# First layer as seven block products in place of eight, in chunks 1 to 8 of a pooled-attention and four-expert kernel

## The chip, the cores and the metric

The kernel runs on one core of one Trainium2 chip. The metric is device time in microseconds (us) of one execution, lower is better. Times are medians of several executions. Engines are named as in the profile: PE is TensorE (matmuls), DVE VectorE, ACT ScalarE, POOL GpSimd, SP the engine that issues many of the DMAs.

## The reference, cut to what matters

```python
# attention: q, k, v are 8 x 8 x 576 x 64; keys and values are averaged by 8, so 72 of each
k_p = k.reshape(B, H, 72, 8, D).mean(axis=3);  v_p = v.reshape(B, H, 72, 8, D).mean(axis=3)
attn_out = softmax(q @ k_p.T / sqrt(D)) @ v_p
x = attn_out.transpose(0, 2, 1, 3).reshape(4608, 512)
# four experts, p = normalized domain_probs
for e in range(4):
    h = np.maximum(x @ w1[e], 0.0)            # "first layer":  4608x512 @ 512x1024
    out += p[:, e:e+1] * (h @ w2[e])          # "second layer": 4608x1024 @ 1024x512
```

The kernel cuts the 4608 tokens into nine chunks of 512: the first 512 tokens of each of the eight batches, and a ninth chunk (chunk 8) of what remains of all batches. A pair (chunk, expert) has one first and one second layer. While the layers of chunk c run, the attention of batch c+1 is worked in between them.

## The kernel before: the parts that the change touches

The second layer is already done as 7 block products in place of 8: each operand is cut into four quarters, seven products of sums of quarters are made, and the results are added with the right signs. The sums of quarters of H (the hidden layer) are made on DVE. The first layer is plain: 32 matmuls of 128x512.

```python
    def up(c, e, fcs, at=slice(0, NT)):                    # first layer, 4 matmuls for each fc
        ...
        for fc in fcs:
            h_ps = psum_h.tile([P, NT], F32, name="h_ps")
            out_ps = h_ps[:, 0:at.stop - at.start]
            for kc in range(KC):
                nc.tensor.matmul(out_ps, lhsT=w1_bf[:, e, kc, fc*P:(fc+1)*P], rhs=xT[:, kc, at], ...)
            nc.scalar.activation(out=H_sb[:, fc, at], in_=out_ps, func=ACT.Relu)

    def down(c, e, step):                                  # second layer, one of 7 products
        a11, a12, a21, a22 = quarters(c, e)
        ...
            lambda: (0, False, a11, w[:, LO, 0:HD], 0, 0, True),
            lambda: (1, False, a12, w[:, HI, 0:HD], 0, 0, False),
            lambda: (0, True, state["S2"], t[:, 1], 0, 1, True),     # the third needs a sum of H
            ...
        # 8 matmuls of 128x256, then add(): acc = p_e * PSUM + acc on DVE (ACT for e == 0)

    def turn(b, r):                                        # x of a batch, transposed by a DMA
        ...
        if b:
            nc.sync.dma_start_transpose(out=dst, in_=x_tok)
            return
        ...                                                # batch 0 alone: transposed on PE

    def next_loads(b):                                     # loads of the next batch
        ...
        turned = state[("kpT", b)][0:1, 0, 0:1] if b >= BUSY else state[("xT", b)][0:1, 0, NT - 1:NT]
        nc.gpsimd.tensor_copy(out=gate[0:1, 0:1], in_=turned)   # holds the queue until x is turned
        load_q(b + 1); load_k(b + 1); load_v(b + 1); load_q_rem(b + 1)
```

The one-element copy called `gate` matters later: it makes the GpSimd queue, which issues the loads, wait until the last transposed x of batch 1 has landed before it loads batch 2. (In the kernel before, POOL waited 35.71 us for `xT<-x_tok`, ran the copy at 75.24 and issued the first of these loads at 75.75.)

The softmax here doesn't subtract the row's maximum and nothing guards it: scores larger than these inputs give would overflow.

## Time and profile before

| | before |
|---|---|
| time, median of 3 runs | 531.21 us (530.46 to 531.53) |
| PE busy | 510.8 us of a span of 528.7 (97%) |
| DVE / ACT / POOL busy | 66% / 46% / 8% |
| DVE in a 55-us window in the middle | 39 us |
| one first layer (32 matmuls 128x512) | 32 x 0.2165 = 6.93 us |

The page of the kernel before gives the busy time of each engine and the shares of the chain of waits that ended last, by engine and by line. L450 is the first layer, L524 the second.

```profile
span 528.7 us, 9160 instructions
PE 510.8 (97%) x3735; PEld 332.7 (63%) x3802; DVE 348.8 (66%) x715; ACT 240.8 (46%) x413; POOL 40.0 (8%) x57
...
PE 87%; DVE 9%; DMA 1%; issue 1%; ACT 1%; DVEq 0%; POOL 0%; POOLq 0%
```

PE is the limit. The next lines, from the PE timeline of the kernel before (start, duration, engine, line, operation, operands, how many), show what a narrow matmul costs.

```profile
216.43 1.04 PE L450 MATMUL h_ps<-xT,w_bf 128*128 128x512 bf16 x4
217.30 1.04 PE L524 MATMUL o_ps<-w_bf,H_sb 128*128 128x256 bf16 x8
218.18 0.81 PE L450 MATMUL h_ps<-xT,w_bf 128*128 128x512 bf16 x3
```

From start to start, four matmuls of 512 columns take 0.87 us (216.43 to 217.30) and eight of 256 columns 0.88 us (217.30 to 218.18). A matmul with half the columns takes half the time, about 0.109 us.

The windows of the kernel before give busy time in stretches of the run (columns: busy us of PE, weight loads, DVE, ACT, POOL with instruction counts, then the granted TensorE clock, the DMA share and GB/s). The first is the start of chunk 1, the second the steady state.

```profile
75.00:101.00 26.00, 25.04 (x169) 16.64 (x171) 22.15 (x42) 11.31 (x21) 4.10 (x7) 1.00 0.81 141
...
211.00:266.00 55.00, 54.36 (x400) 36.12 (x406) 39.03 (x80) 25.99 (x45) 4.46 (x5) 1.00 0.55 87
```

PE has about half a microsecond to spare in 55.

To compare stretches of the two runs I use a marker: the start of the third product of a second layer, which is the same in both kernels and recurs once in each layer. These lines of the PE timeline of the kernel before are the first matmul of chunk 1, then the marker beside the first layer of chunk 1, expert 0 (I call this step 0), beside that of expert 1 (step 1), and in the very last second layer (step 32).

```profile
75.32 1.02 PE L450 MATMUL h_ps<-xT,w_bf 128*128 128x512 bf16 x4
...
80.40 1.03 PE L524 MATMUL o_ps<-wt_bf,S_943 128*128 128x256 bf16 x8 [0.79 <-DVE acc L556]
...
93.41 1.04 PE L524 MATMUL o_ps<-wt_bf,S_1081 128*128 128x256 bf16 x8
...
517.10 1.03 PE L524 MATMUL o_ps<-wt_bf,S_5909 128*128 128x256 bf16 x8 [0.91 <-DVE acc L556]
```

### The profile page before, as it was taken

The numbers are of one execution on the slowest core, as the hardware profiler recorded it, in microseconds if no ns is written. First come the engines' busy times: TensorE is split into PE (matmuls) and PEld (weight loads), VectorE is DVE, ScalarE is ACT, GpSimd is POOL, SyncE is SP. The second block draws the span as 40 slices with busy tenths as digits, with TensorE's granted clock in tenths as the row PEclk, the third lists the DMA queues.
The fourth block names the chain that finished last, engine by engine and source line by source line (L and its number), as shares of the span: only waits on it lengthen the run. The fifth ranks groups of instructions, "written<-read, shape, count | busy, mean of one in ns | idle before, by whom it ended". The sixth has DMA issues, their size and how long they took to land.

```text
span 528.7 us, 9160 instructions
## 1 busy us (share of the span) xinstructions
PE 510.8 (97%) x3735; PEld 332.7 (63%) x3802; DVE 348.8 (66%) x715; ACT 240.8 (46%) x413; POOL 40.0 (8%) x57
## 2 busy tenths in 40 slices
PE   8999999999999999999999999999999999999994
PEld 4656456666666666666666666666666666666663
DVE  4432687977866767677857784778477636664665
ACT  2665413653365335633563347334733363336330
POOL 6420020200030002000300002000000000000000
PEclk9999999999999999999999999999999999999999
DMA  9999939673192125912671329232010110010002
GB/s 188 210 210 204 141 59 204 92 109 61 31 194 33 31 51 125 115 30 51 137 92 30 61 93 123 44 60 86 9 21 20 50 41 12 0 47 36 1 0 79
DMA packets 73417, 42.02 MB, mean 79 GB/s; under 512 B 44688, under 2 KB 67216, under 8 KB 73376
## 3 DMA queue, kind: packets, MB, share of 16 engines
q0 software_dynamic: 30976, 22.11, 29.2%
q1 hardware_dynamic: 42080, 18.82, 14.8%
q8 instruction: 29, 0.48, 0.4%
q10 hardware_dynamic: 320, 0.52, 0.3%
q14 instruction: 12, 0.10, 0.1%
HBM read 45.16 MB, written 9.44 MB: 103 GB/s over the span
## 4 chain that ended last, share of the span: by engine, by line
PE 87%; DVE 9%; DMA 1%; issue 1%; ACT 1%; DVEq 0%; POOL 0%; POOLq 0%
PE h_ps L450 42%; PE o_ps L524 37%; DVE acc L556 3%; PE o_ps L541 2%; PE sc_ps L262 2%; PE c_ps L290 1%; DMA kraw<-in_k_dram 1%; DVE kraw L174 1%; PE s_ps L205 1%; DVE kraw L176 1%; DVE wt_bf L469 1%; PE w_ps L221 1%; DVE x_tok L279 1%; DVE kp_100 L184 0%; ACT expT L265 0%
## 5 line engine op out<-in xcount | busy, mean ns | idle before, releaser
L454 ACT ACTIVATE H_sb<-h_ps 128x512 bf16<-128x512 f32 (+1 forms) x296 | 173.2, 585 | 242.3 <-PE h_ps L450 226.6
L556 DVE SCALAR_TENSOR_TENSOR acc<-o_ps,p_all,acc 128x256 f32<-128x256 f32 (+1 forms) x412 | 181.8, 483 | 125.9 <-PE o_ps L524 96.1
L450 PE MATMUL h_ps<-xT,w_bf 128*128 128x512 bf16 (+1 forms) x998 | 253.2, 372 | 3.2 <-ACT xT L308 0.4
L450 PEld LDWEIGHTS <-w_bf 128*128 128x128 bf16 x1184 | 112.0, 98 | 85.0 <-issue 5.3
L524 PEld LDWEIGHTS <-H_sb 128*128 128x128 bf16 x816 | 79.8, 98 | 33.3 <-issue 3.4
L524 PE MATMUL o_ps<-w_bf,H_sb 128*128 128x256 bf16 x544 | 70.3, 273 | 1.4 <-DVE acc L556 1.2
L554 ACT ACTIVATE acc<-o_ps,p_all 128x256 f32<-128x256 f32 x72 | 30.7, 470 | 12.4 <-PE o_ps L524 7.2
L524 PE MATMUL o_ps<-wt_bf,H_sb 128*128 128x256 bf16 x272 | 35.2, 272 | 0.6 <-DVE acc L556 0.3
L265 ACT ACTIVATE expT<-sc_ps 72x1024 bf16<-72x1024 f32 x32 | 31.0, 1015 | 6.6 <-PE sc_ps L262 6.6
L450 PE MATMUL h_ps<-x_rem,w_bf 128*128 128x512 bf16 x121 | 31.7, 379 | 0.3
L279 DVE TENSOR_TENSOR x_tok<-c_ps,inv 128x512 bf16<-128x512 f32 x36 | 24.9, 691 | 1.2
L541 PE MATMUL o_ps<-w_bf,H_sb 128*128 128x512 bf16 x63 | 14.7, 379 | 0.1
L290 PEld LDWEIGHTS <-expT 72*128 72x128 bf16 x256 | 12.1, 98 | 1.7 <-DVE x_tok L279 0.2
L221 PE MATMUL w_ps<-zeros 128*128 128x512 bf16 x41 | 11.7, 425 | 1.2 <-DVE zeros L574 1.2
L541 PEld LDWEIGHTS <-H_sb 128*128 128x128 bf16 x64 | 6.1, 98 | 7.1
L278 DVE RECIPROCAL inv<-c_ps 128x8 f32<-128x8 f32 x36 | 7.1, 198 | 5.2 <-PE c_ps L343 2.9
L427 POOL COPY gate<-kpT_101 1x1 bf16<-1x1 bf16 x2 | 1.5, 736 | 96.9 <-DMA kpT_101<-kp_99 55.3
L174 DVE TENSOR_TENSOR kraw<-kraw 72x2048 bf16<-72x2048 bf16 x7 | 8.5, 1210 | 0.0
L174 DVE TENSOR_TENSOR vraw<-vraw 72x2048 bf16<-72x2048 bf16 x7 | 8.5, 1210 | 0.0
L89 POOL DMA_DIRECT2D kraw<-in_k_dram x9 | 7.6, 841 | 5.1 <-PE h_ps L450 4.7
L221 PEld LDWEIGHTS <-zeros 128*128 128x128 bf16 x42 | 4.1, 108 | 5.7 <-issue 2.3
L89 POOL DMA_DIRECT2D vraw<-in_v_dram x9 | 7.1, 795 | 0.7 <-DVE vp_106 L226 0.7
(489 smaller groups left out, 467.8 us busy)
## 6 DMA issues: line engine op xcount, KB each, us to landing
out_dram<-acc SPq DMA_DIRECT2D x32, 256.0 KB, 2.7
w_bf<-in_moe_w_dram POOLq DMA_DIRECT2D x7, 1024.0 KB, 22.5
kraw<-in_k_dram POOLq DMA_DIRECT2D x7, 576.0 KB, 12.3
vraw<-in_v_dram POOLq DMA_DIRECT2D x7, 576.0 KB, 14.2
q_sb<-in_q_dram POOLq DMA_DIRECT2D x7, 512.0 KB, 7.0
acc<-in_q_dram SPq DMA_DIRECT2D x2, 512.0 KB, 4.3
w_bf<-in_moe_w_dram POOLq DMA_DIRECT2D x2, 512.0 KB, 12.0
kraw<-in_k_dram POOLq DMA_DIRECT2D x2, 288.0 KB, 7.4
```

Of the source, the lines that this page charges most:

```text
L89: nc.gpsimd.dma_start(out=raw[:, hs], in_=src[b, hs].rearrange("h (j r) d -> j h r d", r=POOL))
L174: nc.vector.tensor_add(out=raw[:, hs, 0:4, :], in0=raw[:, hs, 0:4, :], in1=raw[:, hs, 4:8, :])
L221: nc.tensor.matmul(w_ps[:], lhsT=zeros[:, 0:P], rhs=zeros[:])
L265: nc.scalar.activation(out=expT[:, 2 * pair:2 * pair + 2].rearrange("j h a b t -> j b (h a) t"), in_=sc_ps[0:SP].rearrange("j b h (a t) -> ...
L279: nc.vector.tensor_tensor(out=x_tok[:], in0=c[:, :, :, 0:D], in1=inv[:].unsqueeze(3).to_broadcast([P, 2, NPAIR, D]), op=ALU.mult,)
L290: nc.tensor.matmul(c_ps[:, h // NPAIR, at:at + D + 1], lhsT=expT[:, h, r // 2, r % 2, :], rhs=vp[:, h, :],)
L450: nc.tensor.matmul(out_ps, lhsT=w1_bf[:, e, kc, fc * P:(fc + 1) * P], rhs=xT[:, kc, at], start=(kc == 0), stop=(kc == KC - 1),)
L454: nc.scalar.activation(out=H_sb[:, fc, at], in_=out_ps, func=ACT.Relu)
L524: nc.tensor.matmul(o_ps, lhsT=lhs[:, i, j * P:(j + 1) * P], rhs=rhs[:, i, :], start=(not grows and i == 0 and j == 0), stop=(i == HF - 1), ...
L541: nc.tensor.matmul(o_ps[:], lhsT=H_sb[:, fc, r * P:(r + 1) * P], rhs=w2_bf[:, e, fc, :], start=(fc == 0), stop=(fc == FCH - 1),)
L554: nc.scalar.activation(out=dst, in_=o_ps, func=ACT.Copy, scale=prob)
L556: nc.vector.scalar_tensor_tensor(out=dst, in0=o_ps, scalar=prob, in1=dst, op0=ALU.mult, op1=ALU.add,)
```

## The change

The intent is to save PE time: the first layer too becomes 7 products of blocks, 56 matmuls of 128x256 in place of 32 of 128x512, for the 32 pairs of chunks 1 to 8. The price is sums of blocks: four sums of x for each chunk, sixteen sums of w1 once, and relu of a sum of two products, which is made in one custom VectorE operation, relu(PSUM + SBUF), after ACT has copied the first product out of PSUM. To make room on DVE, two of the seven products of a second layer (steps 1 and 4) are accumulated by ACT and POOL, and the folding of k and v, from batch 2 on, is left to loads in four parts that add up in memory. H lives in two buffers by quarters, the buffers of x by tokens go from 4 to 3, and the `gate` is gone. The core of the diff:

```diff
+    def relu_sum(dst, ps, part):
+        nc.vector._custom_dve(TENSOR_ADD_SAT, out=dst, in0=ps, in1=part, s0=LARGEST, s1=0.0)
+
+    def up_product(c, e, unit, step):          # two units of two PSUM banks each
+        a11, a12, s3, a22 = weight_parts(e)
+        b11, t3, b21, b22 = x_parts(c)
+        s, t = wu_bf[:, e], state[("xs", c)]
+        bank, grows, lhs, rhs = [
+            (0, False, a11, b11),
+            (1, False, a12, b21),
+            (0, True, s[:, 1], t[:, 1]),       # the third needs a sum of x and a sum of w1
+            ...
+        ][step]
+        # 4 matmuls of 128x256
+        if step == 0 or step == 3:
+            nc.scalar.copy(out=part[:, 0], in_=ps)
+        elif step == 2:
+            nc.scalar.copy(out=part[:, 1], in_=ps)
+        elif step == 1:
+            relu_sum(quarter(0, 0), ps, part[:, 0])
+        ...
     def down(...):
+        if step in pooled and e > 0:
+            for j in range(BLOCKS):
+                nc.scalar.activation(out=addend[:, j], in_=ps[:, j], func=ACT.Copy, scale=prob)
+            nc.gpsimd.tensor_add(out=dst, in0=dst, in1=addend[:])
+    def load_part(b, part):
+        ...
+            if part:
+                nc.gpsimd.dma_start(out=raw[:], in_=rows, accum_op=ALU.add)
...
-        x_tok = npool.tile([P, 2, NPAIR, D], BF16, name="x_tok", bufs=4)
+        x_tok = npool.tile([P, 2, NPAIR, D], BF16, name="x_tok", bufs=3)
...
-        nc.gpsimd.tensor_copy(out=gate[0:1, 0:1], in_=turned)
...
+        sums = {(0, 2): lambda: first_weight_sums(0), (0, 7): lambda: weight_sums(0),
+                (1, 6): lambda: first_weight_sums(1), (2, 6): lambda: first_weight_sums(2),
+                (3, 5): lambda: first_weight_sums(3), (3, 7): lambda: weight_sums(3)}
...
+            if s == 2:
+                load_part(2, 1)
+            if s == 3:
+                load_q(2)
+                load_part(2, 2)
...
+        x_sums(1)
+        load_part(2, 3)
+        sums = {(0, 6): lambda: weight_sums(1), (1, 6): lambda: weight_sums(2)}
+        POOLED = (1, 4)
+        for g in range(7 * (N + 1) + 1):       # slots: 2 first-layer products, 1 second-layer product
+            t, i = divmod(g, 7)
+            if t < N:
+                up_product(*order[t], 0, i)
+            t2, i2 = divmod(g - 1, 7)
+            if 0 <= t2 < N:
+                up_product(*order[t2], 1, i2)
+            if g >= 1 and t2 <= N:
+                down(*below_of[t2], i2, t2 % 2, POOLED)
+            ...                                # hidden sums at i = 0, 1, 2; attention by slot
```

## The prediction

> **What bounds it now.** TensorE. The page gives PE 510.8 us busy of 528.7 (97%) at full granted clock; the chain of waits puts 87% of the span on PE lines, 42% on the first layer's matmuls and 37% on the second's. From the first matmul of chunk 1 (75.3 us) to the last first-layer matmul of chunk 8 (514.3) the timeline shows 54.9 us per chunk, and 55-us windows show 53.9 to 54.6 us of PE busy. DVE has 38 to 42 us in such a window, ACT 26, POOL at most 7.5.
>
> **Removed.** In the timeline four 128x512 matmuls take 0.866 us and eight 128x256 ones 0.870 us, so a 256-column product runs at 0.109 us: narrower matmuls cost nothing extra here (weight loads of 98 ns stay hidden, barely). A first layer falls from 32 x 0.2165 = 6.93 us to 56 x 0.1088 = 6.09 us, 0.84 us for each of 32 layers: about 27 us, all on the critical path. PE alone would give 504 us.
>
> **Added and moved, per chunk.** DVE gains six PSUM+SBUF relu sums for each layer. It is a custom operation with no duration in this trace; I take that of the 128x512 multiply-add out of PSUM, 748 ns, less the 0.09 us overlap seen between neighbours: 0.66 us. [...] My sum for three layers: 6 x 0.66 + 4 bf16 sums x 0.65 + 10 accumulations x 0.39 = 10.5 us; the first layer has 6 accumulations, 8.9 us; attention 6.5 us with sums of x, less the folding that accumulating DMAs take over. Total about 47 us of the expected 53: DVE goes from some 72% to about 90%. ACT goes to about 30 us (copies at 0.5 us), not a limit. POOL gets six 128x512 additions. [...]
>
> **Where it is given back.** A slot is 1.74 us of PE (two first-layer products and one second-layer product). At each turn of layer DVE has, in order: last relu, two accumulations, two hidden sums, a relu, two accumulations, then the S2 sum that the third second-layer product needs. Counted from durations above, S2 is ready about 6.2 us after the turn and PE asks at 6.1. So small stalls, about 0.2 us, and 0.7 to 1 us more in the turn where a context division (0.9 us) comes before S2, or where x sums meet a GpSimd addition. I put 1 to 2 us per chunk back (8 to 16 us), and 3 to 5 us once for weight sums of the first layer (16 x 0.69 us on DVE, partly in the overlapped prologue), the start of chunk 1 and the tail. Chunks 53 us, total 516 us (-2.9%).
>
> **Range.** 505 to 527 us, 8 in 10. Faster by over 2%: 0.72; within 2%: 0.26; slower: 0.02.
>
> **What would show it.** Right: chunk period 52 to 54 us; first-layer matmuls 256 wide at 0.109 us; PE busy near 480 us; DVE over 80%; new PE waits mostly on DVE (S2, relu sums), at the third second-layer product. Relu sum 0.7 to 0.8 us.
>
> **What would make it wrong.** A custom operation that costs over 0.9 us pushes DVE past PE (each 0.1 us is 4.8 us of DVE per chunk): then about 530 us. GpSimd additions that lock DVE out for over 1 us each. Accumulating DMAs landing late, so that POOL and with it the addend buffer and ACT wait. On the other side, if slack absorbs the turn stalls, 506 us.

The sum stays at 504 us of PE, 8 to 16 us given back in the chunks and 3 to 5 us once, for a stated total of 516 us (at their middles the terms add to 520, as said at the end). What the text says of x sums that meet an addition and a DVE that is locked out was the author's estimate; the kernel after shows one such sum at 1.49 us, against a mean of 417 ns in d1, which has no POOL additions.

## The result, and the profile after

The changed kernel took 533.39 us (median of 4 runs, 532.70 to 534.13); the kernel before, in the same rounds, 530.84 us (529.89 to 531.53). The ratio is 1.0047 with a 95% interval of 1.003 to 1.0064: within 2%, and if anything slower. A ratio here is always the mean time of one kernel's fast runs over that of the other's of the same rounds, so it is not quite the ratio of the medians. The predicted 516 us and its range of 505 to 527 missed.

The page of the kernel after, the lines that answer to those of before:

```profile
span 530.9 us, 11431 instructions
PE 499.8 (94%) x4562; PEld 407.0 (77%) x4570; DVE 435.4 (82%) x830; ACT 274.1 (52%) x513; POOL 156.2 (29%) x137
...
PE 71%; DVE 12%; DMA 11%; ACT 2%; issue 2%; SPq 0%; DVEq 0%; ACTq 0%
```

PE is busy for less time, as intended, but its share of the chain has fallen from 87% to 71%, and DMA has 11% of the chain where it had 1%. The same two windows of the kernel after:

```profile
75.00:101.00 26.00, 19.25 (x164) 14.48 (x162) 21.27 (x39) 7.86 (x14) 8.59 (x8) 0.87 0.90 91
...
211.00:266.00 55.00, 53.12 (x517) 45.45 (x517) 49.34 (x94) 29.84 (x56) 20.44 (x17) 1.00 0.68 79
```

In the steady window PE now lacks 1.9 us of 55 (before 0.6), and DVE has gone from 39 to 49 us. In the start window PE lacks 6.75 us of 26, and the granted clock was 0.87.

What PE waited for, in the kernel after (total us, times, longest):

```profile
PE o_ps L566 <- DVE S L187: 9.1, 12, 1.7
PE unit L500 <- DMA xT<-x_tok: 4.8, 1, 4.8
PE unit L500 <- DVE xs L187: 1.9, 1, 1.9
PE unit L500 <- ACT partial L514: 1.8, 2, 1.3
...
```

How long the four transposing DMAs of batch 1's x took from issue to landing, from the view of the tile `xT` (60 to 95 us), first in the kernel before, then in the kernel after:

```profile
DMA to landing us min/median/max: 2.5/2.5/2.5
...
DMA to landing us min/median/max: 3.7/8.8/9.0
```

L566 is the second layer, and its wait for `S` is at the marker, the third product. L500 is the new first layer. The PE timeline of the kernel after, at the start of chunk 1 and at the markers of steps 0, 1 and 32:

```profile
81.33 2.72 PE L500 MATMUL unit<-xT,w_bf 128*128 128x256 bf16 x12 [4.81 <-DMA xT<-x_tok]
...
87.05 0.61 PE L500 MATMUL unit<-xs,wu_bf 128*128 128x256 bf16 x4 [1.94 <-DVE xs L187]
...
91.34 1.04 PE L566 MATMUL o_ps<-wt_bf,S 128*128 128x256 bf16 x8
...
106.44 1.05 PE L566 MATMUL o_ps<-wt_bf,S 128*128 128x256 bf16 x8 [0.78 <-DVE S L187]
...
517.47 1.63 PE L566 MATMUL o_ps<-wt_bf,S 128*128 128x256 bf16 x8 [1.68 <-DVE S L187]
```

Now the run can be cut into three parts by the markers:

| part | before | after | difference |
|---|---|---|---|
| start: to the marker of step 1 | 93.41 | 106.44 | +13.0 |
| steady: step 1 to step 32, 31 layers | 423.69 | 411.03 | -12.7 |
| tail: step 32 to the end of the span | 11.6 | 13.4 | +1.8 |
| span of the profiled run | 528.7 | 530.9 | +2.2 |

(The tail is the span less the marker: 528.7 - 517.10 and 530.9 - 517.47. The three differences add to +2.1; the rest is rounding. The start holds one new first layer too, so its +13.0 is already net of 0.84 us.) So the layers did become faster, by about half of the 26 us that 31 layers of 0.84 us should give, and the start and the tail gave that back. The tail's 1.8 us seem to belong to this execution: behind the wait of 1.68 us the granted clock was 0.56 (517.47 to 520 us) and eight matmuls took 1.63 us, while the runs a1 to a3 and b1 to b3 below have the same wait of 1.68 us at this marker and then 1.05 us; in a1, for example, the tail is 11.7 us.

The relu sum, the one cost that had to be guessed, is in the groups of the kernel after (busy us, mean ns, idle before), by form, with four groups that will matter:

```profile
L481 DVE CUSTOM_DVE_ANT_0 H<-unit,partial 128x512 bf16<-128x512 f32 x192 | 130.7, 683 | 25.5 <-PE unit L500 12.6 <-ACT acc L601 11.8 <-ACT H L520 0.2
L187 DVE TENSOR_TENSOR S<-H 128x1024 bf16<-128x1024 bf16 x68 | 46.4, 682 | 0.3
L187 DVE TENSOR_TENSOR H<-H,S 128x1024 bf16<-128x1024 bf16 x34 | 32.3, 951 | 0.5 <-DVE S L187 0.5
...
L221 DVE TENSOR_TENSOR kp<-kraw 72x512 bf16<-72x512 bf16 x12 | 8.8, 772 | 0.0
```

It costs 683 ns, as hoped: less than the 748 ns of the 128x512 multiply-add out of PSUM in the kernel before, from which it had been estimated.

Two operations of the same shape, `S<-H` and `H<-H,S`, take 682 and 951 ns. Some DVE sums took longer beside a POOL addition. The DVE and POOL timeline of the kernel after, at one turn from a chunk to the next, shows such meetings:

```profile
249.23 1.54 POOL L577 TENSOR_TENSOR acc<-acc,addend 128x512 f32<-128x512 f32 x1 [4.36 <-DVE xs L187]
...
249.56 1.49 DVE L187 TENSOR_TENSOR xT<-xT 128x512 bf16<-128x512 bf16 x1
...
255.99 0.87 DVE L603 SCALAR_TENSOR_TENSOR acc<-o_ps,p_all,acc 128x256 f32<-128x256 f32 x2
256.77 0.68 DVE L187 TENSOR_TENSOR S<-H 128x1024 bf16<-128x1024 bf16 x1
257.03 1.56 POOL L577 TENSOR_TENSOR acc<-acc,addend 128x512 f32<-128x512 f32 x1 [6.26 <-DVE acc L603]
257.37 1.83 DVE L221 TENSOR_TENSOR kp<-kraw 72x512 bf16<-72x512 bf16 x2
...
257.51 1.05 PE L566 MATMUL o_ps<-wt_bf,S 128*128 128x256 bf16 x8 [0.95 <-DVE S L187]
```

The sum `xT<-xT` took 1.49 us beside a POOL addition, and the pair `kp` 1.83 us. In d1 below, which has no POOL additions, the means are 417 ns for `xT<-xT`, 415 for one `kp` and 678 for `H<-H,S`. Some texts call this lengthening exclusion; what is shown is the longer time, not how it comes about. DVE works almost without a gap from 249.2 to 257.5; the sum S arrives 0.95 us after PE wanted it. Two things are ahead of it that may not need to be: about 1.1 us that `xT<-xT` took beyond its mean in d1, and accumulations of the second layer.

### The profile page after: what moved, and what is told of

It reads as the page before. It is cut to its first block, busy times and chain, and to the rows that moved or that the text cites. A ratio compares the mean times of both kernels' runs of the same rounds, so it can differ in the third digit from the quotient of the medians.

```text
span 530.9 us, 11431 instructions
## 1 busy us (share of the span) xinstructions
PE 499.8 (94%) x4562; PEld 407.0 (77%) x4570; DVE 435.4 (82%) x830; ACT 274.1 (52%) x513; POOL 156.2 (29%) x137
## 4 chain that ended last, share of the span: by engine, by line
PE 71%; DVE 12%; DMA 11%; ACT 2%; issue 2%; SPq 0%; DVEq 0%; ACTq 0%
PE o_ps L566 30%; PE unit L500 28%; DMA xT<-x_tok 6%; DMA out_dram<-acc 5%; PE unit L448 5%; DVE acc L603 4%; DVE H L481 2%; PE unit L256 2%; DVE S L187 2%; PE o_ps L590 1%; PE att L300 1%; DVE xs L187 1%; PE att L326 1%; DVE wt_bf L187 1%; ACT expT L304 1%
## 5 line engine op out<-in xcount | busy, mean ns | idle before, releaser
L481 DVE CUSTOM_DVE_ANT_0 H<-unit,partial 128x512 bf16<-128x512 f32 x192 | 130.7, 683 | 25.5 <-PE unit L500 12.6
L577 POOL TENSOR_TENSOR acc<-acc,addend 128x512 f32<-128x512 f32 x50 | 69.4, 1387 | 278.2 <-ACT addend L575 197.8
L566 PEld LDWEIGHTS <-H 128*128 128x128 bf16 x1360 | 134.0, 99 | 18.5 <-issue 0.9
L512 ACT COPY partial<-unit 128x512 f32<-128x512 f32 x128 | 74.9, 585 | 112.2 <-PE unit L500 86.4
L500 PEld LDWEIGHTS <-w_bf 128*128 128x128 bf16 x1024 | 98.8, 98 | 23.4 <-issue 6.0
L566 PE MATMUL o_ps<-w_bf,H 128*128 128x256 bf16 x816 | 106.8, 274 | 0.3 <-DVE acc L603 0.3
L500 PE MATMUL unit<-xT,w_bf 128*128 128x256 bf16 x672 | 98.1, 276 | 7.4 <-DMA xT<-x_tok 4.8
L500 PEld LDWEIGHTS <-wu_bf 128*128 128x128 bf16 x768 | 73.0, 98 | 13.1 <-issue 2.5
L500 PE MATMUL unit<-xs,wu_bf 128*128 128x256 bf16 x512 | 77.1, 273 | 1.9 <-DVE xs L187 1.9
L566 PE MATMUL o_ps<-wt_bf,H 128*128 128x256 bf16 x544 | 71.4, 275 | 0.1
L566 PEld LDWEIGHTS <-S 128*128 128x128 bf16 x544 | 52.1, 99 | 20.7 <-DVE S L187 13.9
L514 ACT COPY partial<-unit 128x512 f32<-128x512 f32 x64 | 38.0, 594 | 21.3 <-PE unit L500 21.2
L566 PE MATMUL o_ps<-wt_bf,S 128*128 128x256 bf16 x272 | 36.0, 276 | 9.1 <-DVE S L187 9.1
L500 PE MATMUL unit<-xs,w_bf 128*128 128x256 bf16 x256 | 38.5, 273 | 0.0
L566 PE MATMUL o_ps<-w_bf,S 128*128 128x256 bf16 x272 | 35.5, 274 | 0.1
L500 PE MATMUL unit<-xT,wu_bf 128*128 128x256 bf16 x224 | 33.7, 273 | 0.0
```

The source lines that it names most:

```text
L481: nc.vector._custom_dve(TENSOR_ADD_SAT, out=dst, in0=ps, in1=part, s0=LARGEST, s1=0.0)
L500: nc.tensor.matmul(ps[:, n * HN:(n + 1) * HN], lhsT=lhs[:, kc, f:f + P], rhs=rhs[:, kc, :], start=(not grows and n == 0 and kc == 0), stop ...
L512: nc.scalar.copy(out=part[:, 0], in_=ps)
L514: nc.scalar.copy(out=part[:, 1], in_=ps)
L566: nc.tensor.matmul(ps[:, j], lhsT=lhs[:, i, j * P:(j + 1) * P], rhs=rhs[:, i, :], start=(not grows and i == 0 and j == 0), stop=(i == HF - 1),
L577: nc.gpsimd.tensor_add(out=dst, in0=dst, in1=addend[:])
```

## The experiments

The questions: (1) what makes the start late: the fewer buffers of x by tokens, the accumulating loads, loads in flight at all, or DVE's backlog of weight sums? (2) what eats half of the steady gain: S late on DVE because POOL additions lengthen DVE's sums and because of the order of work, or the stores? My theory for the start was that the transposing DMAs of x land late because loads of batch 2 are in flight, the rival that a smaller buffer count or DVE is to blame. In the list, each experiment changes the kernel after. The kernel before took 530.9 to 531.5 us (medians) in the rounds of the experiments.

### a1: four buffers of x by tokens

```diff
-        x_tok = npool.tile([P, 2, NPAIR, D], BF16, name="x_tok", bufs=3)
+        x_tok = npool.tile([P, 2, NPAIR, D], BF16, name="x_tok", bufs=4)
```

> The changed kernel with 4 x_tok buffers instead of 3 (before had 4). At the start of chunk 1 the fourth x_tok waited 5.2 us for the transposing DMA of the first one, and PE was idle 4.8 us. Buffer theory: the missing buffer is the cause, so the 5.2 us wait and most of the 4.8 us of PE idle vanish, -4 to -5 us (about 529). Rival, slow landing theory: the transposes land late (8.8 us against 2.5 before) because accumulating loads of batch 2 are in flight; then the fourth transpose starts earlier but also lands late, and the time falls by 0 to 2 us.

Measured: 531.95 us (529.20 to 533.06), ratio to before 1.0016 (0.9978 to 1.0054). The PE timeline of this run shows the start no earlier:

```profile
82.11 2.72 PE L500 MATMUL unit<-xT,w_bf 128*128 128x256 bf16 x12 [5.62 <-DMA xT<-x_tok]
```

DVE's wait for a buffer of x by tokens (5.2 us in the kernel after) is gone, and in its place DVE waits 5.2 us in all for the transposed x itself, ahead of the sums of x. The buffer wait was only a symptom of the late landing, and the buffer theory falls.

### a2: x of batch 1 transposed on PE

```diff
-        if b:
+        if b > 1:
             nc.sync.dma_start_transpose(out=dst, in_=x_tok)
             return
-        xt_ps = spare_bank()...
+        xt_ps = one_bank(b)...
```

> The x of batch 1 is transposed on PE through PSUM instead of by DMA, so that no transfer stands between attention and chunk 1. Slow landing theory: the 4.8 us of PE idle vanish, the first first-layer product starts near 77 instead of 81.3 us, minus 1.6 us of PE for 16 transposes; next it waits for the sums of x behind weight sums on DVE, so -3 to -6 us. Rival (DVE backlog alone sets the start): the third product still starts near 87 us and the time stays within 1 us.

Measured: 536.19 us (535.49 to 539.20), ratio 1.0112 (1.0082 to 1.0142): slower, a miss. The DMA wait was gone, but the four transposes now stood among PE's matmuls and each waited for its x on DVE (1.03 to 1.25 us each); the third product started at 92.44, after 3.57 us of waiting for the sums of x. DVE itself was behind. So taking the DMA away does not repair the start alone, and since it put new waits on PE, this run is no clean test of the landing.

### a3: stores by quarters

In the kernel after, a row of the output is stored after steps 5 and 6, when all of it is done, and the next chunk's first write to `acc` waits for that. Here each half is stored as soon as it is final.

```diff
-        if e == E - 1 and step in (5, 6):
-                store(c, row * BLOCKS + j)
+        if e == E - 1 and step in (1, 4, 5, 6):
+                store(c, row * BLOCKS + j, cols)
```

> Results are stored by column halves as soon as each is final, so the store that ACT's first write of the next chunk waits for (4.3 us in six waits in the trace, 1.6 us longest) is issued four steps earlier. Theory: ACT's wait for the store delays the copies of partial sums and so PE (1.3 us idle in chunk 4, 0.5 us in chunk 1); expected: these waits vanish, -2 to -5 us. Rival (the waits are hidden by other waits of the same turn of layer): no change[...].

Measured: 531.78 us (531.37 to 535.19), ratio 1.0032 (1.0 to 1.0064). The waits of ACT for the stores fell from 4.3 to 1.9 us, while PE's waits for S grew. Its median is 1.6 us below that of the kernel after, in other rounds. The stores are a small part of it.

### a4: POOL takes steps 4 and 6 in place of 1 and 4

```diff
-        POOLED = (1, 4)
+        POOLED = (4, 6)
```

> GpSimd takes the accumulations of steps 4 and 6 instead of 1 and 4: DVE has two accumulations fewer before the S2 sum at each turn of layer and two more after it. Order-of-DVE theory: the PE waits for S (9.1 us named, each some 0.16 us longer than named) shrink below 3 us, -4 to -8 us. Rival (exclusion between GpSimd additions and DVE sums is what makes DVE late): the additions of step 6 now fall onto the S sums themselves, waits for S stay or grow, time the same or up.

Measured: 526.15 us (525.52 to 527.94), ratio 0.9917 (0.9897 to 0.9937), with the same number of POOL additions. The window and two groups of this run:

```profile
156.00:211.00 55.00, 55.00 (x541) 47.74 (x540) 48.62 (x97) 33.03 (x61) 21.52 (x18) 1.00 0.65 77
```

```profile
L187 DVE TENSOR_TENSOR H<-H,S 128x1024 bf16<-128x1024 bf16 x34 | 23.1, 678 | 0.0
...
L221 DVE TENSOR_TENSOR kp<-kraw 72x512 bf16<-72x512 bf16 x12 | 4.5, 415 | 0.0
```

PE is busy in the whole window, and the slow forms are back at 678 ns (from 951) and 415 ns (from 772). This one line does two things: the POOL additions now lengthen DVE's sums by 5.8 us in place of 16.8 (worked out under d1), and the two accumulations of step 6 leave DVE just before the sum S is due. The runs don't separate the shares of the two.

### d1: no POOL accumulation at all

```diff
-        POOLED = (1, 4)
+        POOLED = ()
```

> The changed kernel without GpSimd additions: DVE does all accumulations (1.6 us more for each of three layers, 4.7 us per chunk, some 56 us of DVE per chunk: more than PE needs), and no DVE sum is held by GpSimd. If the exclusion costs more than the additions save, the time falls below 531; if DVE load and order decide, it rises to 540 to 555 us, with PE waits on DVE in every layer.

Measured: 562.06 us (557.20 to 565.07), ratio 1.0544 (1.0477 to 1.061). With no additions on POOL, `H<-H,S` took 678 ns, `xT<-xT` 417, `kp<-kraw` 415 and `xs<-xT,xs` 421, while the relu sum (681, in the kernel after 683) and the 128x256 accumulations (474, there 475), which read one operand from PSUM, stayed as they were. This gives what the POOL additions cost DVE in the kernel after: 34 x (951-678) + 12 x (772-415) + 7 x (724-417) + 14 x (497-421) ns = 16.8 us of DVE over the run, from the means of the two runs. In the same way a4 has 5.8 us. But without POOL's help DVE is overloaded: accumulations are late, so stores are late, so the next chunk waits at its first write. The ACT and the PE timeline of this run at a turn of chunk:

```profile
229.47 0.47 ACT L601 ACTIVATE acc<-o_ps,p_all 128x256 f32<-128x256 f32 x1 [4.46 <-DMA out_dram<-acc]
...
231.51 0.80 PE L500 MATMUL unit<-xT,w_bf 128*128 128x256 bf16 x4 [4.50 <-ACT partial L514]
```

So POOL's additions are worth having; where they fall decides what they cost.

### b1: only the first quarter of batch 2's k and v is loaded (wrong result)

```diff
-            if s == 2:
-                load_part(2, 1)
-                load_part(2, 2)
-        load_part(2, 3)
```

> Wrong result on purpose: of batch 2, only the first quarter of k and v is loaded; the three accumulating pairs of loads that were in flight at the start of chunk 1 are left out (batches 3 to 7 as in the changed kernel). Slow landing theory: the transposing DMAs of x land in about 2.5 us as before instead of 8.8, PE idles under 1 us instead of 4.8 and chunk 1 starts near 77; then the sums of x wait for the weight sums on DVE (ready near 83 instead of 87.6), -4 to -6 us in all. Rival (DVE backlog alone): start of the third product stays near 87, under -1 us.

Measured: 532.92 us (531.01 to 535.05), ratio 1.004 (1.0002 to 1.0078). The first line below is from the view of the tile of transposed x (stretch of batch 1), the others from the PE timeline of this run:

```profile
DMA to landing us min/median/max: 2.4/2.5/2.7
```

```profile
82.82 1.04 PE L500 MATMUL unit<-xs,wu_bf 128*128 128x256 bf16 x4 [3.58 <-DVE xs L187]
...
160.32 0.91 PE L500 MATMUL unit<-xT,w_bf 128*128 128x256 bf16 x4 [2.19 <-ACT partial L514]
...
161.88 1.91 PE L566 MATMUL o_ps<-wt_bf,S 128*128 128x256 bf16 x8
```

The landing is 2.5 us as in the kernel before (2.5), against a median of 8.8 in the kernel after, and PE no longer waits for a DMA. So the loads in flight do cause the late landing. (In d1 and e2 the profile puts the first product's wait of 5.67 and 3.46 us down to DVE, to a different operation in each that ended just then; the transposes landed late there too, with medians of 9.8 and 7.6 us.) The third product moved from 87.05 to 82.82, and the rest of the start is DVE's: 3.58 us of waiting for the sums of x. The total did not fall, against the expected 4 to 6 us. In the profiled execution, one of two near 535 us (the other two took 531.4 and 531.0), stores at two turns of chunk were late (7.0 us of store waits on ACT against 4.3) and cost two PE waits of about 2.2 us, with a granted clock of 0.83 from 155 to 165 us, around the first, behind which eight matmuls took 1.91 us in place of 1.04. Why the stores fell worse here was not looked into further.

### b2: b1 with the weight sums spread over later layers (wrong result)

```diff
-                (3, 5): lambda: first_weight_sums(3), (3, 7): lambda: weight_sums(3)}
+                (3, 7): lambda: weight_sums(3)}
-        sums = {(0, 6): lambda: weight_sums(1), (1, 6): lambda: weight_sums(2)}
+        sums = {(0, 3): lambda: weight_sums(1), (1, 3): lambda: weight_sums(2),
+                (2, 3): lambda: first_weight_sums(3)}
```

> As the run without the three pairs of loads (wrong result on purpose), and the weight sums of the first layer of expert 3 and two of the second layer move from the turns of layer to the fourth slot of the layers, where DVE has room. If both the late landing and the DVE backlog hold the start: a further -2 to -4 us against that run, sums of x ready near 80 us, and the S waits of chunk 1 (0.8 us each) shrink. If the landing alone holds it: within 1 us of that run.

Measured: 529.43 us (528.82 to 530.67), ratio 0.9981 (0.9961 to 1.0001). The third product began at 81.08, 1.7 us earlier than in b1. The sums of w1 of the last expert, queued on DVE ahead of the sums of x, are the second part of the late start.

### b3: parts loaded without accumulation (wrong result)

```diff
-                nc.gpsimd.dma_start(out=raw[:], in_=rows, accum_op=ALU.add)
+                nc.gpsimd.dma_start(out=raw[:], in_=rows)
```

> Wrong result on purpose: all partial loads write instead of accumulate; same bytes, same number of loads and waits. If accumulation itself makes the loads slow (7.1 to 7.8 us each in the median), they land sooner, transposes too, and the time falls 3 to 6 us; if it is the bytes and packets in flight (twice as many packets as before), the landing times and the time stay within 1 us.

Measured: 531.14 us (530.13 to 531.61), ratio 1.0003 (0.9985 to 1.002). PE started chunk 1 at 81.03 after 5.05 us of waiting for the DMA, much as in the kernel after (81.33 after 4.81), and the transposes landed in 8.2 us in the median (8.8 there). So it is not the adding that delays the transposes, it is the loads' being in flight, which the `gate` used to prevent. The parts themselves landed sooner without adding (those of k in 5.5 us against 7.1).

### c1: a4, a3 and the spread weight sums together

> Correct result. GpSimd takes steps 4 and 6, stores by column halves, weight sums moved to the fourth slot. The first alone gave 526.2 us. If the store wait and the weight sums each hold PE where the S sum no longer does: -4 to -8 us more, 518 to 522 us. Rival (they are hidden behind the start): within 1.5 us of 526.

Measured: 525.77 us (525.17 to 526.68), ratio 0.9906 (0.9888 to 0.9924): hardly better than a4 alone. Four weight sums in one block hold DVE up for 2.7 us, and the relu sums behind them made PE wait 1.75 and 1.40 us in the first layers of chunk 1. In the profiled runs c1 reached the marker of step 1 at 104.45, against 107.67 in a4, but its steady part was 1.1 us and its tail 1.4 us longer; the blocks are one cause of that, the rest was not traced.

### e2: a4 and a3

> Correct result. Steps 4 and 6 on GpSimd plus stores by halves; weight sums and buffers as in the changed kernel. a4_pool46 alone gave 526.15 us and still had PE waits of 0.6 and 0.2 us on ACT's copies. If the store wait still costs PE there: 523.5 to 525.5 us. If it is hidden once DVE is early: 525.5 to 526.7 us.

Measured: 525.66 us (525.16 to 527.82), ratio 0.9886 (0.9867 to 0.9904), the same as a4 within the spread. Once DVE is early, the store wait is hidden and a3 is worth nothing.

### c2 and c3: weight sums one at a time, with and without the gate

Both have a4 (with the last second layer left at steps 1 and 4), a3, a1, and the weight sums one to a slot. c2 also puts the gate back before the last two parts of batch 2, and moves batch 2's attention later to match.

```diff
-                (3, 5): lambda: first_weight_sums(3), (3, 7): lambda: weight_sums(3)}
+                (3, 7): lambda: weight_sums(3)}
...
-        sums = {(0, 6): lambda: weight_sums(1), (1, 6): lambda: weight_sums(2)}
+        sums = {}
+        for p in range(4):
+            sums[(0, 3 + p)] = lambda p=p: weight_sums(1, (p,))
+            sums[(1, 3 + p)] = lambda p=p: weight_sums(2, (p,))
+            sums[(2, 3 + p)] = lambda p=p: first_weight_sums(3, (p,))
-                down(*below_of[t2], i2, t2 % 2, POOLED)
+                down(*below_of[t2], i2, t2 % 2, POOLED if t2 < N else (1, 4))
```

```diff
 # c2 alone
         x_sums(1)
+        nc.gpsimd.tensor_copy(out=gate[0:1, 0:1], in_=state[("xT", 1)][0:1, 0, NT - 1:NT])
+        load_part(2, 2)
         load_part(2, 3)
```

> Correct result. GpSimd takes steps 4 and 6 (1 and 4 in the last layer), stores by halves, 4 x_tok buffers, weight sums one at a time in slots 3 to 6 of the first three layers, and the last two quarters of batch 2 are held back by a tiny copy that reads x of batch 1 (the gate of the kernel before), with attention of batch 2 later in chunk 1. If late landing and DVE backlog set the start and chunk 1: chunk 1 starts near 77 us, third product near 80, and chunk 1 takes 53 to 55 us instead of 59; 512 to 517 us. Rival (what is left is DVE work that has to be done somewhere in chunk 1): 520 or more.

> As the gated version without the gate and without the later attention. The landing theory expects chunk 1 to start near 81 to 82 us, 4 to 5 us later than gated, and the sum 517 to 521 us. If the gate does not matter: within 1 us of the gated one.

Measured: c2 520.67 us (520.48 to 520.98), ratio 0.9796 (0.9775 to 0.9818); c3 520.75 us (520.40 to 522.66), ratio 0.9804 (0.9777 to 0.9832). The gate does what it should for the start: in c2 PE began chunk 1 at 78.32 after waiting only 1.24 us, against 81.68 after 4.61 us in c3 (the transposes landed in 4.9 us in the median, against 8.7), and the marker of step 1 came at 98.93 against 103.64. But with the loads held back, batch 2's attention came late: from the marker of step 1 to that of step 5, chunk 1 took 59.59 us in c2 and 55.60 in c3. The gate moved the loss. In c3, the sum S of step 3 was late, and the PE timeline shows what followed:

```profile
133.11 1.86 PE L566 MATMUL o_ps<-wt_bf,S 128*128 128x256 bf16 x8 [2.06 <-DVE S L187]
```

These eight matmuls took 1.86 us in place of 1.04; the granted clock of the window from 101 to 156 us was 0.97, and 1.00 in the later windows up to 486 us. The length of the wait alone does not decide this: after 2.05 us in e1 eight such matmuls took 1.05 us, and after 1.68 us at the last marker 1.63 in the kernel after but 1.05 in a1.

### c4: c3 with the weight sums one layer earlier

```diff
-                (3, 7): lambda: weight_sums(3)}
+                (3, 7): lambda: (weight_sums(3), weight_sums(1))}
-            sums[(0, 3 + p)] = lambda p=p: weight_sums(1, (p,))
-            sums[(1, 3 + p)] = lambda p=p: weight_sums(2, (p,))
-            sums[(2, 3 + p)] = lambda p=p: first_weight_sums(3, (p,))
+            sums[(0, 3 + p)] = lambda p=p: weight_sums(2, (p,))
+            sums[(1, 3 + p)] = lambda p=p: first_weight_sums(3, (p,))
```

> Correct result. As c3_all_ungated (520.8 us), but the second layer's weight sums of expert 1 run in the 3.5 us that DVE idles before chunk 1, and the other two blocks one layer earlier, so none is left in the third layer. If DVE work limits chunk 1: the 2.1 us wait for S at the last layer of chunk 1 and the lower clock after it vanish, -2 to -4 us, 517 to 519 us. Rival (something else holds chunk 1): within 1 us of 520.8.

Measured: 517.09 us (516.23 to 518.10), ratio 0.9731 (0.9708 to 0.9753), a correct result and the fastest correct version, faster than both kernels. The PE waits, a window and two markers of this run:

```profile
PE unit L500 <- DMA xT<-x_tok: 6.0, 1, 6.0
PE o_ps L566 <- DVE S L187: 2.4, 2, 1.4
```

```profile
211.00:266.00 55.00, 55.00 (x529) 47.61 (x527) 46.91 (x93) 33.17 (x63) 21.03 (x17) 1.00 0.78 85
```

```profile
104.97 1.05 PE L566 MATMUL o_ps<-wt_bf,S 128*128 128x256 bf16 x8 [1.07 <-DVE S L187]
...
502.62 1.05 PE L566 MATMUL o_ps<-wt_bf,S 128*128 128x256 bf16 x8 [1.36 <-DVE S L187]
```

From step 1 to step 32 the 31 layers take 397.65 us, 26.0 less than before, as much as the products should give. That this agrees to the tenth is luck: in the same stretch the waits that the profile names for PE are 3.6 us in the kernel before and 1.4 in c4, so some 2 us of the 26.0 are waits. The start is still 11.6 us later than before, and the tail is 13.7 us (span 516.3).

### e1: c3 without batch 2's later parts (wrong result)

> Wrong result on purpose: c3_all_ungated with the three accumulating pairs of batch 2 left out, as in b1_no_parts2. If late landing costs the start 4 to 5 us and no later wait gives it back here: 516 to 517 us. If an earlier start is always given back in chunk 1: 519.5 to 521 us.

Measured: 516.07 us (515.56 to 516.52), ratio 0.971 (0.9694 to 0.9727), 4.7 us below c3, which differs only in those loads (it ran in other rounds; the ratios differ by 0.9%). Two lines of its PE timeline:

```profile
76.28 1.47 PE L500 MATMUL unit<-xT,w_bf 128*128 128x256 bf16 x12
...
99.41 1.05 PE L566 MATMUL o_ps<-wt_bf,S 128*128 128x256 bf16 x8 [1.07 <-DVE S L187]
```

The marker of step 1 came 4.2 us earlier than in c3 (103.64). So with DVE out of the way, the late landing costs the start between 4 and 5 us by itself. It is not the whole start: 99.41 is 7.0 us before the kernel after, and still 6.0 us behind the kernel before. In this stretch PE's named waits are all on DVE: 2.11 us for the sums of x, 1.19 and 1.07 us for S. A correct version that has both (no late landing and no late attention of batch 2) was not found in these runs.

### Chunk times of the main runs

The times of the other runs stand in their sections. The chunk times below are from the marker of step 1 to that of step 5, 5 to 9 and so on to 29, so they hold chunks 1 to 7; chunk 7 has little attention beside it.

| | us | ratio to before | chunk times by the markers |
|---|---|---|---|
| before | 530.84 | | 56.95 55.61 55.14 55.61 55.13 54.42 53.01 |
| after | 533.39 | 1.0047 | 54.43 54.87 55.77 54.82 52.60 53.36 49.30 |
| a4 | 526.15 | 0.9917 | 55.99 52.61 52.41 52.99 51.68 52.61 49.23 |
| c2 | 520.67 | 0.9796 | 59.59 52.69 51.68 52.62 53.44 52.61 49.16 |
| c3 | 520.75 | 0.9804 | 55.60 53.27 51.68 52.62 51.68 52.61 49.17 |
| c4 | 517.09 | 0.9731 | 51.69 52.79 51.68 52.62 51.68 52.61 49.16 |

## Why the prediction was wrong, point by point

- **What bounds the kernel: right.** PE, as the page and the windows say.
- **What the products save: right.** A matmul of 256 columns stayed at 0.109 us. The prediction said 0.84 us for each layer, 26.0 us for 31 of them, all on the critical path; c4 shows a steady part 26.0 us shorter (423.69 - 397.65), of which some 2 us are waits, as said there.
- **The cost on each engine: right.** The relu sum took 683 ns (the prediction reckoned with 0.66 us beside its neighbours and expected to see 0.7 to 0.8). DVE came to 49.34 us of a 55-us window, 90%, and 82% of the span; ACT to 30 us in that window.
- **Back-payment in the steady part: right in kind, in sum within its range, wrong in how it is spread.** The prediction had S late on DVE, by 0.2 us as a rule and by 0.7 to 1 us where sums of x meet a POOL addition, 8 to 16 us in all. After against c4, the steady part lost 13.4 us (411.03 - 397.65). In the middle chunks the S waits are 0.95 us at the turn of chunk and 0.49 in another layer. By the chunk table the loss is 2.7, 2.1, 4.1 and 2.2 us in chunks 1 to 4, under 1 us in the later ones. Between 107 and 502 us the PE waits that the profile names add to 9.5 us (S 6.6, partial 1.3, expT 1.0, H 0.6). The windows of the two steady parts split the 13.4: PE lacks 11.75 us in the kernel after and 1.67 in c4, which makes 10.1 of it; for the other 3.3 us PE is busy longer (399.28 against 395.98 us) with the same matmuls. Each wait also ends the overlap of about 0.17 us that neighbouring groups show (1.04 us long, 0.87 apart); for the 16 more waits that is about 2.7 us, an estimate. Because c4 changes a4, a3, a1 and the weight sums at once, it shows the size of the loss, and a4 shows that most of it beyond chunk 1 is the place of the POOL additions.
- **"3 to 5 us once for weight sums of the first layer (...), the start of chunk 1 and the tail": this is the step that failed.** It measured 14.8 us: 13.0 at the start and 1.8 in the tail, and the latter seems to be the lowered clock of this one execution, as said with the table. What the prediction had wrong is the overlap: it expected new PE waits mostly on DVE and the weight sums partly hidden in the prologue, and had no wait for a transposing DMA. The start divides so: the first matmul of chunk 1 came at 81.33 in place of 75.32 (6.0 us later, of which 4.81 are the wait for the DMA), the next part to the marker of step 0 took 10.0 us in place of 5.1 (a lowered clock, 0.50 from 81.3 to 84.1: 12 matmuls show 2.72 us where b1's same group shows 1.47; and 1.94 us for the sums of x), and the step from there to the marker of step 1 took 15.1 in place of 13.0. The prediction saw the weight sums, and did not see that the `gate`, which the change removed, had kept the transposes of x clear of other loads (landing 2.5 us before, 8.8 after). b1 shows that the loads delay the landing, b3 that the adding is not the reason, a1 that the buffers are not, e1 that it is worth between 4 and 5 us; b2 shows that the queue of weight sums is the next part (1.7 us at the third product). With both changed, and a4, a3 and a1 besides, e1 wins back 7.0 of the 13.0 us. Of the other 6.0, 4.4 us are named waits for DVE (the kernel before has 0.8 there); the rest is not split, and no run removes it.
- **The arithmetic of the prediction.** Its own terms, at their middles, add to 504 + 12 + 4 = 520 us, not 516. With the measured terms in their place, the profiled span comes out: 528.7 - 26.0 + 13.4 + 13.0 + 1.8 = 530.9; this must come out, since the terms are differences of the same markers, and is no further proof. A slip besides, which did not matter at 683 ns: with six relu sums for each layer a chunk has 24, so 0.1 us more for each would be 2.4 us of DVE per chunk and not 4.8.
- **"PE busy near 480 us" was no good test.** It measured 499.8, but even c4, with the whole steady gain, has 494.6. A matmul at a lowered clock counts as busy for longer (12 took 2.72 us at a granted clock of 0.50, against 1.47 in b1, as above); how much of the difference that is was not measured. And the busy time of the kernel before reads low: its page has 1184 weight loads of L450 but only 1119 matmuls, so some matmul records are missing.
- **The danger that was named, additions on POOL that hold DVE up: half right.** They cost 16.8 us of DVE over the run, in the worst meetings over 1 us each (`xT<-xT` 1.49 us against 417 ns), but d1 shows that taking them off POOL is far worse (562.06 us). The other danger named, accumulating loads that land late and hold up POOL and ACT, came near the cause but named another wait: what the loads held up was the transposes, and b3 shows the same without accumulation.

## What to carry to other kernels

When PE is the limit and a change takes work off it, cost the one-time parts (the first chunk, the last layer) from the trace as carefully as the steady part: here the estimate for the layers was right in the main and the start lost 13 us. Before removing something that looks like a leftover, such as a one-element copy that holds a queue back, ask which transfers it kept apart. On an engine that is 90% full, look at the place of an operation relative to the sum that PE needs next, and to a GpSimd addition, and not only at its duration: here one line that moved two accumulations won about 7 us.
